# SwiGLU feed-forward: the first gate tile loaded in two halves, one on ACT beside the x transpose, one on SP behind it

## Chip, cores and metric

One core of one Trainium2 chip. The metric is the device time of one execution in microseconds (us). The profile's span (first to last instruction) is some 1.8 us shorter than that time.

## The reference

```python
B, S, D, F = 1, 2048, 512, 1376          # x: (B,S,D); w_gate, w_up: (D,F); w_down: (F,D); all bfloat16
def reference(x, w_gate, w_up, w_down):
    g = silu(x @ w_gate)
    u = x @ w_up
    return (g * u) @ w_down
```

## The kernel before

Everything is computed from a transposed x, so that the features lie on partitions. A "tile" of a weight is 128 of its F columns, held as four slices (dk 0 to 3) of 128 features each, 128 KB in bfloat16. x is taken in four chunks of 512 rows, 512 KB each, which the DMA transposes on the way in. For each chunk and tile, TensorE does four matmuls for the gate and four for the up product (128x128 weights, 512 columns), ACT takes the SiLU of the first, DVE multiplies. Ten matmuls on constants come ahead of all that, to bring TensorE's clock up while the first loads are under way.

The loads, in order of issue; `load_w` takes a range of slices:

```python
N_WARM = 10
...
def load_w(eng, w, base, f0, f1, k0=0, k1=KD): ...   # slices k0..k1 of columns f0..f1, one DMA
...
o = load_x("sp", 0)                       # 512 KB, DMA transpose
for dk in range(KD):
    got_x[0, dk] = o
for a, b in ((0, 1), (1, 2), (2, 4), (4, 7), (7, NFT)):
    g = load_w("act" if a == 0 else "sp", w_gate, 0, a * P, min(b * P, F))
    u = load_w("sp", w_up, UPH, a * P, min(b * P, F - 32))
    for ft in range(a, b):
        for dk in range(KD):
            got_g[ft, dk], got_u[ft, dk] = g, u
# ... rest of up, x chunks 1 to 3, w_down: all on SP
op("act", lambda e: e.activation(adummy[:, 0:4], zero_c, ACT.Silu), inc=False)
for i in range(N_WARM):
    op("pe", lambda e: e.matmul(banks[7][:, :], lhsT=ones_w, rhs=ones_m, start=True, stop=True), inc=False)
...
def mm_g(n, c, ft, dk):
    deps = [got_x[c, dk], got_g[ft, dk]]
    if dk == 0 and n >= NG:
        deps.append(silus[n - NG])
    return mm_k(psG[n % NG], ft * P, c, dk, deps)     # mm_u likewise, with got_u
```

So the first gate tile goes out whole on ACT at the same moment as the x transpose on SP; everything else follows x on SP.

## Time and profile before

| | before |
|---|---|
| time, median of 3 runs | 122.46 us (122.28 to 122.61) |
| span of the profiled run | 120.4 us |
| TensorE busy | 116.4 us, 97% |
| DMA engines busy | in the first 24 us, then only stores |
| first real matmul | 5.18 us after the span's start |

The chain of waits that ended last says what the time is made of (columns: start in us, length in us, what):

```profile
...
0.73 4.40 DMA xT_sb<-in_x_dram
...
5.18 72.69 PE bank L165 x336
...
79.73 38.21 PE bank L246 x187
...
```

Once x has landed at 5.14 us, matmul follows matmul to the end: 336 for gate and up in 72.69 us, which is 216 ns each. A change of the loads can move the time only through the start at 5.18 us, or by making holes just after it.

The timeline before the first matmuls (start, length, engine, line, operation; for SPq and ACTq the length is that of the issue, not of the transfer):

```profile
...
0.73 1.41 SPq L123 DMA_TRANSPOSE xT_sb<-in_x_dram  x1
0.74 0.42 ACTq L131 DMA_DIRECT2D w_sb<-in_w_gate_dram  x1
...
0.77 3.65 PE L162 MATMUL bank<-const-bfloat16-1.0 128*128 128x512 bf16 x10 [0.77 <-PEq L301]
...
2.00 0.15 PEld L162 LDWEIGHTS bank<-const-bfloat16-1.0 128*128 128x128 bf16 x1 [0.28 <-issue]
2.20 0.91 SPq L131 DMA_DIRECT2D w_sb<-in_w_up_dram  x1
2.43 0.15 PEld L162 LDWEIGHTS bank<-const-bfloat16-1.0 128*128 128x128 bf16 x1 [0.27 <-issue]
...
3.17 0.49 SPq L131 DMA_DIRECT2D w_sb<-in_w_gate_dram  x1
...
5.18 4.06 PE L165 MATMUL bank<-xT_sb,w_sb 128*128 128x512 bf16 x18 [0.77 <-DMA xT_sb<-in_x_dram]
...
6.26 0.60 ACT L184 ACTIVATE sg_sb<-bank 128x512 f32<-128x512 f32 x1 [3.57 <-PE bank L165]
...
7.99 0.60 ACT L184 ACTIVATE sg_sb<-bank 128x512 f32<-128x512 f32 x1 [1.13 <-PE bank L165]
...
```

The first SP issue behind x took 0.91 us, the later ones about 0.5. Weight loads (PEld) come one per matmul: those of the warm-up are first 0.43 us apart (2.00, 2.43, ...), and by the end 0.22, so TensorE's clock rose to its full rate near 3.4 us. The SiLUs of the first tiles, at 6.26 and 7.99, are 1.73 us apart, eight matmuls at 216 ns: no hole.

In the DMA view of single issues, the gate tile on ACT landed 2.4 us after its issue (3.14 us), x 4.4 us after (5.14), the first up tile 3.5 us after, the second gate tile at 6.16. The gate tile is there two microseconds before it can be used.

### The profile page before, as it was taken

The page shows a single profiled execution, that of the slowest core. Times are in us where ns is not written, and L with a number is a line of the kernel's source. Part 1 is how long each engine was busy: PE and PEld are TensorE (multiplying, and loading weights), DVE is VectorE, ACT ScalarE, POOL GpSimd, SP SyncE. Part 2 cuts the span into 40 slices and gives each one's busy share as a digit, 9 for nine tenths or more (in the row PEclk, how much of TensorE's full clock was granted, in tenths as well). Part 3 has the DMA queues.
Part 4 walks back from the last instruction along what each step waited for, and adds up shares of the span by engine and source line. Part 5 has one row for each costly group of instructions (what it writes and reads, how often), then busy time and mean ns, then how long its engine had stood idle before and what let it go on. Part 6 is the DMA issues. An engine that isn't in the chain of part 4 may idle for free.

```text
span 120.4 us, 1381 instructions
## 1 busy us (share of the span) xinstructions
PE 116.4 (97%) x549; PEld 53.0 (44%) x549; DVE 43.8 (36%) x64; ACT 30.2 (25%) x51; POOL 0.2 (0%) x4
## 2 busy tenths in 40 slices
PE   7799999999999999999999999999999999999991
PEld 2244444444444444444444444444444444444470
DVE  0024433444433444433444433466332233224230
ACT  4033233353233363233363233320000000000001
POOL 0000000000000000000000000000000000000000
DMA  3999999900000000000000000000211211121121
GB/s 82 270 299 369 264 227 288 306 4 0 0 0 0 0 0 5 0 0 3 3 0 0 0 0 0 5 0 0 87 44 44 87 44 46 58 75 44 44 74 57
DMA packets 17990, 8.51 MB, mean 71 GB/s; under 512 B 11360, under 2 KB 17984, under 8 KB 17984
## 3 DMA queue, kind: packets, MB, share of 16 engines
q1 hardware_dynamic: 17312, 8.23, 25.0%
q10 hardware_dynamic: 672, 0.20, 0.7%
q8 instruction: 4, 0.07, 0.3%
q14 instruction: 2, 0.02, 0.1%
HBM read 4.23 MB, written 2.10 MB: 53 GB/s over the span
## 4 chain that ended last, share of the span: by engine, by line
PE 94%; DMA 4%; ACT 0%; issue 0%
PE bank L165 60%; PE bank L246 32%; DMA xT_sb<-in_x_dram 4%; PE bank L220 2%; ACT o_sb L253 0%
## 5 line engine op out<-in xcount | busy, mean ns | idle before, releaser
L165 PE MATMUL bank<-xT_sb,w_sb 128*128 128x512 bf16 x336 | 72.7, 379 | 0.8 <-DMA xT_sb<-in_x_dram 0.8
L165 PEld LDWEIGHTS bank<-xT_sb,w_sb 128*128 128x128 bf16 x336 | 32.8, 98 | 40.7 <-DMA xT_sb<-in_x_dram 1.3
L187 DVE TENSOR_TENSOR hT_sb<-sg_sb,bank 128x512 bf16<-128x512 f32 x40 | 27.5, 688 | 44.7 <-PE bank L165 44.6
L246 PE MATMUL bank<-wd_sb,hT_sb 128*128 128x512 bf16 (+3 forms) x187 | 38.3, 366 | 0.0
L184 ACT ACTIVATE sg_sb<-bank 128x512 f32<-128x512 f32 x40 | 23.8, 596 | 43.5 <-PE bank L165 43.5
L246 PEld LDWEIGHTS bank<-wd_sb,hT_sb 128*128 128x128 bf16 (+1 forms) x187 | 18.2, 98 | 20.2 <-issue 0.4
L254 DVE CAST o_sb<-bank 128x512 bf16<-128x512 f32 (+1 forms) x16 | 10.8, 674 | 23.7 <-PE bank L246 23.7
L253 ACT ACTIVATE o_sb<-bank 128x256 bf16<-128x256 f32 x1 | 0.4, 384 | 38.9 <-PE bank L246 38.9
L211 DVE TENSOR_TENSOR hT_sb<-sgx_sb,bank 32x512 bf16<-32x512 f32 x4 | 2.8, 693 | 4.9 <-ACT sgy_sb L209 4.9
L162 PE MATMUL bank<-const-bfloat16-1.0 128*128 128x512 bf16 x10 | 3.6, 538 | 0.8 <-PEq L301 0.8
L208 ACT ACTIVATE sgx_sb<-bank 32x512 f32<-32x512 f32 x4 | 2.4, 588 | 4.5 <-PE bank L165 4.5
L226 DVE TENSOR_TENSOR hT_sb<-sgy_sb,bank 64x512 bf16<-64x512 f32 x4 | 2.7, 685 | 0.1
L162 PEld LDWEIGHTS bank<-const-bfloat16-1.0 128*128 128x128 bf16 x10 | 1.2, 131 | 2.7 <-issue 2.6
L209 ACT ACTIVATE sgy_sb<-bank 64x512 f32<-64x512 f32 x4 | 2.4, 589 | 0.0
L220 PE MATMUL bank<-xT_sb,w_sb 128*64 128x512 bf16 x16 | 1.9, 382 | 0.0
L158 ACT ACT_TABLE_LOAD x1 | 1.3, 1283 | 1.2 <-PEq L301 1.2
L220 PEld LDWEIGHTS bank<-xT_sb,w_sb 128*64 128x64 bf16 x16 | 0.8, 109 | 1.0 <-issue 0.4
L158 ACT ACTIVATE act_dummy<-const-float32-0.0 128x4 f32<-128x4 f32 x1 | 0.2, 206 | 0.0
L301 POOL MEMSET const-bfloat16-1.0<- 128x1 bf16 x1 | 0.1, 101 | 0.0
L301 POOL MEMSET const-uint8-127<- 128x1 uint8 x1 | 0.1, 101 | 0.0
L301 POOL MEMSET const-float32-0.0<- 128x1 f32 x1 | 0.1, 98 | 0.2 <-issue 0.2
L301 POOL MEMSET const-float32-1.0<- 128x1 f32 x1 | 0.1, 98 | 0.0
## 6 DMA issues: line engine op xcount, KB each, us to landing
out_dram<-o_sb SPq DMA_DIRECT2D x15, 128.0 KB, 1.7
wd_sb<-in_w_down_dram SPq DMA_DIRECT2D x1, 1280.0 KB, 7.1
w_sb<-in_w_gate_dram SPq DMA_DIRECT2D x1, 480.0 KB, 5.9
w_sb<-in_w_up_dram SPq DMA_DIRECT2D x1, 448.0 KB, 6.0
w_sb<-in_w_gate_dram SPq DMA_DIRECT2D x1, 384.0 KB, 4.6
w_sb<-in_w_up_dram SPq DMA_DIRECT2D x1, 384.0 KB, 5.1
w_sb<-in_w_up_dram SPq DMA_DIRECT2D x2, 128.0 KB, 3.2
w_sb<-in_w_gate_dram SPq DMA_DIRECT2D x1, 256.0 KB, 3.9
```

Of the source, the lines that this page charges most:

```text
L158: op("act", lambda e: e.activation(adummy[:, 0:4], zero_c, ACT.Silu), inc=False)
L162: op("pe", lambda e: e.matmul(banks[7][:, :], lhsT=ones_w, rhs=ones_m, start=True, stop=True), inc=False)
L165: return op("pe", lambda e: e.matmul(bank[:, :], lhsT=w_sb[:, dk, col0:col0 + P], rhs=xT_sb[:, dk, c * SC:(c + 1) * SC], start=(dk == 0), ...
L184: s = op("act", lambda e: e.activation(sg_sb[n % NSG][:, :], psG[n % NG][:, :], ACT.Silu), [g, mults[n - NSG] if n >= NSG else None])
L187: mults.append(op("dve", lambda e: e.tensor_tensor(hT_sb[:, ft, c * SC:(c + 1) * SC], sg_sb[n % NSG][:, :], psU[n % NU][:, :], ALU.mult), ...
L208: op("act", lambda e, c=c: e.activation(sgx_sb[c][96:128, :], psX[64:96, :], ACT.Silu), [xm], inc=False)
L209: rest_a[c] = op("act", lambda e, c=c, y0=y0, y1=y1: e.activation(sgy_sb[c][y0:y1, :], psX[0:64, :], ACT.Silu), [xm])
L211: rest_x[c] = op("dve", lambda e, c=c: e.tensor_tensor(hT_sb[64:96, NFF, c * SC:(c + 1) * SC], sgx_sb[c][96:128, :], psX[96:128, :], ALU.m ...
L220: ym = op("pe", lambda e, pi=pi, dk=dk, c=c, y0=y0, y1=y1: e.matmul(psY[pi][y0:y1, :], lhsT=w_sb[:, dk, YC0:YC0 + 64], rhs=xT_sb[:, dk, c ...
L226: rest_y[c] = op("dve", lambda e, pi=pi, c=c, y0=y0, y1=y1: e.tensor_tensor(hT_sb[0:64, NFF, c * SC:(c + 1) * SC], sgy_sb[c][y0:y1, :], ps ...
L246: om = op("pe", lambda e, K=K, fk=fk: e.matmul(bank[:, 0:ncol], lhsT=hT_sb[0:K, fk, t * P:(t + 1) * P], rhs=wd_sb[0:K, fk, c0:c0 + ncol], ...
L254: return op("dve", lambda e: e.tensor_copy(ob[:, a:b], bank[:, a - c0:b - c0]), deps)
```

## The change

The gate tile's bytes use the same DMA engines as x while x is what TensorE waits for. The intent is to take half of them out of x's way: the half that is needed first (features 0 to 255) stays on ACT, the other half comes on SP right behind x, then the up tile.

```diff
-        for a, b in ((0, 1), (1, 2), (2, 4), (4, 7), (7, NFT)):
-            g = load_w("act" if a == 0 else "sp", w_gate, 0, a * P, min(b * P, F))
+        early = load_w("act", w_gate, 0, 0, P, 0, KD // 2)
+        late = load_w("sp", w_gate, 0, 0, P, KD // 2, KD)
+        up = load_w("sp", w_up, UPH, 0, P)
+        for dk in range(KD):
+            got_g[0, dk], got_u[0, dk] = early if dk < KD // 2 else late, up
+        for a, b in ((1, 2), (2, 4), (4, 7), (7, NFT)):
+            g = load_w("sp", w_gate, 0, a * P, min(b * P, F))
             u = load_w("sp", w_up, UPH, a * P, min(b * P, F - 32))
```

## The prediction

> **What bounds the kernel now.** TensorE. The page gives PE 97% busy; the chain of waits is 94% PE, 4% one DMA: the first x transpose, issued at 0.73 us, landed at 5.14. After 5.18 the chain is unbroken matmul: 336 at the gate/up line in 72.69 us (216 ns each), 16 for the rest in 1.85, 187 down in 38.21. So only the PE start and holes in the first tiles can move.
>
> **What the change does.** The first gate tile (128 KB) goes out today on ACT at 0.74 and lands 2.4 us later, at 3.16 (DMA issues by tile) with 2 us to spare; but its bytes share the DMA engines with x. In the windows table the engines are full (share 1.2 to 1.3, 270 to 290 GB/s) from 2.2 us to 5.8 us. The Trainium skill ("DMA: Bandwidth & Descriptors", section "Issuing engines are not separate DMA queues") says transfers from ACT and SP run on the same 16 engines and interleave; the trace agrees: the total stays near 280 GB/s with and without the ACT transfer. The change takes 64 KB out of x's way and puts it behind x on SP. Estimate: 65.5 kB / 280 GB/s = 0.23 us, so x lands near 4.9 and PE starts near 4.95.
>
> **What it costs.** One more SP issue, 0.49 to 0.51 us (timeline), so every later SP issue moves back about 0.5 us. Deadlines, with four matmuls = 0.865 us and PE starting at 4.95:
> - late half: needed at 4.95 + 0.43 = 5.38. Before, 128 KB behind x landed 0.56 after x (5.70); 64 KB should land 0.3 after it, near 5.2. Slack 0.15 us.
> - first up tile: needed at 5.81. The bytes ahead of it are unchanged, so 5.7. Slack 0.1 us.
> - gate 1, up 1: landed 6.17, 6.60, needed 6.68, 7.55: fine, also 0.3 us later.
> - gates 2 and 3 (256 KB): landed 8.15, needed 8.41. Around 6.0 to 6.4 us the engines are not full (share 0.84, 138 GB/s), so this transfer is probably bound by its issue; if all 0.5 us came through, it would land at 8.65 and open a hole of 0.2 us, giving the gain back.
> - ups 2 and 3: landed 8.9, needed 9.27; a similar risk. Later tiles have over 1 us.
>
> **Sum.** Gain 0.23 us at the start, minus about 0.08 us for the chance that part returns as a hole: 122.46 - 0.15 = 122.3 us. The range, 121.95 to 122.65, is mostly the runs' spread. Faster by over 2%: 1%; within 2%: 98%; slower by over 2%: 1%.
>
> **What would show each step.** (1) x landing at 4.85 to 5.0, its time to landing down from 4.4 to about 4.2 us; (2) first gate/up matmul at 4.9 to 5.05; (3) SP issues from the first up tile on 0.4 to 0.55 us later; (4) the waits list: no PE wait on w_sb of over 0.1 us in the first 1.0 us of matmuls; perhaps one of 0.1 to 0.3 us near 8.4 us for gates 2 and 3; (5) the chain after that the same 112.8 us.
>
> **What would make it wrong.** x may be bound not by the shared engines but by its own issue (1.41 us) and transposing, and then lands at 5.14 as before: no gain, and the late half and up tile have more slack. The late half or the up tile may land later than the byte count says, since the first issue behind x took 0.91 us, not 0.5; each would stall PE by 0.1 to 0.4 us, and the run would be 122.5 to 122.8.

## The result, and the profile after

| | before | after |
|---|---|---|
| time, median | 122.53 us (122.28 to 122.67, 4 runs) | 122.48 us (122.23 to 122.56, 4 runs) |
| ratio | | 0.9995, interval 0.9971 to 1.0018 |
| x lands, us after its issue | 4.4 | 4.0 |
| first real matmul | 5.18 us | 4.99 us |
| first SiLU | 6.26 us | 6.59 us |

A ratio is the mean time of one kernel's runs over that of the other's runs of the same rounds, so not quite the ratio of the medians. Executions over 1.5% slower than the fastest of the same kernel are left out of the means. The interval spans 0.36 us down to 0.22 us up: the two kernels can't be told apart. Yet x landed 0.4 us earlier (the view of x's first issue, after):

```profile
...
DMA to landing us min/median/max: 4.0/4.0/4.0
```

The profiled runs took 122.17 us (before, a run outside the four listed) and 122.56 us (after). The chain of waits after:

```profile
...
0.77 4.43 PE bank L167 x10
5.20 73.01 PE bank L170 x336
...
80.05 38.21 PE bank L251 x187
...
```

The DMA of x has gone from the chain. In its place stand the ten warm-up matmuls, 4.43 us of them, where those of before took 3.65; and the 336 real ones took 73.01 us, not 72.69. The timeline after:

```profile
...
0.73 0.42 ACTq L131 DMA_DIRECT2D w_sb<-in_w_gate_dram  x1
0.73 1.40 SPq L123 DMA_TRANSPOSE xT_sb<-in_x_dram  x1
...
2.19 0.57 SPq L131 DMA_DIRECT2D w_sb<-in_w_gate_dram  x1
...
2.82 0.45 SPq L131 DMA_DIRECT2D w_sb<-in_w_up_dram  x1
...
3.31 0.51 SPq L131 DMA_DIRECT2D w_sb<-in_w_gate_dram  x1
...
4.14 0.15 PEld L167 LDWEIGHTS bank<-const-bfloat16-1.0 128*128 128x128 bf16 x1 [0.28 <-issue]
...
4.99 4.37 PE L170 MATMUL bank<-xT_sb,w_sb 128*128 128x512 bf16 x17
5.42 0.15 PEld L170 LDWEIGHTS bank<-xT_sb,w_sb 128*128 128x128 bf16 x1 [0.28 <-DMA w_sb<-in_w_gate_dram]
...
5.84 0.15 PEld L170 LDWEIGHTS bank<-xT_sb,w_sb 128*128 128x128 bf16 x1 [0.28 <-issue]
...
6.17 2.90 PEld L170 LDWEIGHTS bank<-xT_sb,w_sb 128*128 128x128 bf16 x14 [0.17 <-issue]
6.59 0.60 ACT L189 ACTIVATE sg_sb<-bank 128x512 f32<-128x512 f32 x1 [3.90 <-PE bank L170]
...
8.31 0.60 ACT L189 ACTIVATE sg_sb<-bank 128x512 f32<-128x512 f32 x1 [1.13 <-PE bank L170]
```

Weight loads are still 0.42 us apart at 5.42 and 5.84: in this run TensorE's clock rose near 6.0 us, not near 3.4. So the warm-up matmuls ended only at about 5.0 us, after x, and the first real matmuls ran at half speed. From first matmul to first SiLU it took 6.59 - 4.99 = 1.60 us, before 6.26 - 5.18 = 1.08. The early start gained 0.19 us, the slow clock took 0.52, and the sum, 0.33, is the difference between the two SiLUs and between the two profiles' ends. After that the SiLUs are 1.72 us apart: no hole.

Does the change cause the late rise, or chance? The Trainium skill ("TensorE: Matmul & The Clock Gate", section "What's actually happening") describes a clock gate that goes from half to full rate after a window of about 3.4 us has been busy enough, and says that the window is free-running and does not start with the kernel. The two rates agree with these traces (427 and 216 ns per matmul); that the moment varies from run to run is seen below. The views print a granted clock of 1.00 throughout the first 6 us, but that is no measurement: they print 1.00 wherever the trace has no clock record. The packed trace's own clock records (not shown by a view) begin at 6.06 us here and at 5.67 in the repeat below, where the spacing also puts the rise; the profile of before has none. Eleven of the fourteen traces have such records, and all but the last one of each, cut off by the end, last 3.41, 6.83, 112.64, 116.05 or 119.47 us, each a whole multiple of 3.413, as a free-running window would make them. By these records, or by the spacing where there are none, the rise lay between 3.4 and 6.7 us with the load order of before and with that of the change alike (later only in the run with eight warm-up matmuls), so it is chance and not the change.

The SP issues: the first one behind x took 0.57 us (before 0.91), so the second gate tile was issued at 3.31 us instead of 3.17, 0.14 us later, not 0.5.

### The profile page after: what moved, and what is told of

The parts are those of the page before. It is cut to its first block, busy times and chain, and to the rows that moved or that the text cites. A ratio compares the mean times of both kernels' runs of the same rounds, so it can differ in the third digit from the quotient of the medians.

```text
span 120.8 us, 1382 instructions
## 1 busy us (share of the span) xinstructions
PE 117.5 (97%) x549; PEld 53.4 (44%) x549; DVE 43.8 (36%) x64; ACT 30.2 (25%) x51; POOL 0.2 (0%) x4
## 4 chain that ended last, share of the span: by engine, by line
PE 97%; ACT 0%; issue 0%
PE bank L170 60%; PE bank L251 32%; PE bank L167 4%; PE bank L225 2%; ACT o_sb L258 0%
## 5 line engine op out<-in xcount | busy, mean ns | idle before, releaser
L167 PE MATMUL bank<-const-bfloat16-1.0 128*128 128x512 bf16 x10 | 4.4, 629 | 0.8 <-PEq L306 0.8
```

## Experiments

Theory 1: x does land earlier; the gain is hidden by TensorE's clock. Theory 2: the warm-up matmuls stand in the way. Theory 3: x's earlier landing was chance. And a fourth: the gain comes back as holes. Each run below was made with the kernel before on the same chip. "Held" kernels are an instrument, described with the first of them.

### The changed kernel again

No edit.

> The changed kernel again, unchanged, for more runs. Theory 1 (the gain is real but hidden by the TensorE clock at the start, whose rise to full speed came near 3.4 us in the profile of before and near 6.0 us in the profile of after): runs spread over about 0.5 us, the fastest run near 121.9 (0.4 below the fastest of before, 122.28), the mean 0.15 to 0.25 us below before. Theory 2 (the ten warm-up matmuls at the slow clock, 4.43 us, now end after x has landed and take the gain in every run): fastest run not under 122.15, mean within 0.1 us of before. Theory 3 (x does not land earlier in most runs, the profile of after was lucky): x lands at 5.0 to 5.2 us in this profile.

Measured: 122.08, 122.28, 122.30, 122.32, 122.80, 122.87, mean 122.44 us; before, 11 runs of 122.06 to 123.02, ratio 1.0001 (0.9967 to 1.0035). x landed 4.1 us after its issue, so theory 3 is weakened. The clock rose near 5.7 us, and again the warm-up matmuls (4.42 us) were in the chain. The mean shows no gain, as theory 2 expected, and the fastest run is no faster than before's 122.06 (though 122.08 lies just under the 122.15 that theory 2 allowed); the spread of 0.8 us is more than the 0.5 that theory 1 expected, and before has it too (0.96 us).

### Fewer warm-up matmuls

```diff
-N_WARM = 10
+N_WARM = 8
```

> The changed kernel with 8 warm-up matmuls instead of 10: at the slow clock they end near 4.2 us, ahead of x at 4.73. Theory 1: mean equal to the repeat within 0.1 us. Theory 2: 0.15 us or more below the repeat, PE starts real work at x's landing (4.75 to 4.85 us) whatever the clock. If instead the idle gap delays the clock's rise, the mean is 0.1 us or more above the repeat.

Measured: four fast runs of 121.98, 122.13, 122.49 and 122.99 us, mean 122.40, ratio 0.9996 (0.9956 to 1.0036); two more, 124.15 and 124.55, were slow, and the profile fell in the first of them. The mean of the four equals the repeat's 122.44 within 0.1 us, as theory 1 said; theory 2 asked for 0.15 us less. No comparison of times is taken from the profile, only what it shows of the clock (weight loads after x):

```profile
...
5.25 0.13 PEld L170 LDWEIGHTS bank<-xT_sb,w_sb 128*128 128x128 bf16 x2 [1.82 <-DMA xT_sb<-in_x_dram]
...
8.64 0.15 PEld L170 LDWEIGHTS bank<-xT_sb,w_sb 128*128 128x128 bf16 x1 [0.28 <-issue]
9.06 4.85 PEld L170 LDWEIGHTS bank<-xT_sb,w_sb 128*128 128x128 bf16 x23 [0.27 <-issue]
```

x landed late in this run (4.5 us after issue), TensorE stood idle for 0.92 us after its eight warm-up matmuls, and the weight loads stayed 0.42 us apart until 9.06 us. Theory 2's cure fails in the fast runs, and a hole ahead of the rise can cost more than it saves. An estimate from the traces: counted back in steps of 3.41 us from the rise, the stretch from 2.23 to 5.65 us held the whole 0.92 us of idle time, and without it the rise would have come at 5.65. In the other thirteen traces, counted the same way, the stretches ahead of the rise with up to 0.72 us of idle time were followed by the full clock and those with 0.89 us or more were not. Had x landed at 4.73, the hole would have been 0.4 us and harmless by this count; x was late here (4.5 us after issue).

### The clock taken out: both kernels held back

To take the clock out of the comparison, the x and gate loads wait for four ACT activations, which moves everything by 3.6 us (4.4 had been expected, and so a time near 126.8), and 24 warm-up matmuls keep TensorE busy, so that the clock has risen before x lands. The same edit was made to the kernel before and to the changed one:

```diff
-N_WARM = 10
+N_WARM = 24
+        op("act", lambda e: e.activation(adummy[:, 0:4], zero_c, ACT.Silu), inc=False)   # moved up from below the loads
+        for i in range(4):
+            hold = op("act", lambda e, i=i: e.activation(adelay[:, i, :], ones_m, ACT.Silu))
-                return dma(eng, ... xf[t0:t1, :]))
+                return dma(eng, ... xf[t0:t1, :]), [hold])        # load_w likewise
```

> The kernel before with the first x and gate loads held back about 4.4 us by four ACT activations, and 24 warm-up matmuls, so that in every run the clock has risen before x lands. It takes the clock's lottery away. x lands about 4.4 us after its issue, near 9.5 us; runs near 126.8 us with a spread of under 0.2 us if the clock causes the spread; a spread of 0.4 us as before if it does not.

> The same hold on the changed kernel. Theory 1 and 2: 0.3 to 0.45 us below the held kernel before, x lands 4.0 us after its issue instead of 4.4. Theory 3, or a hole later in the first tiles (late half, up tile, gates 2 and 3): within 0.1 us of it, and in case of a hole a PE wait on w_sb of 0.2 us or more in the waits list.

Measured: held before 125.77 to 125.87 (6 runs, mean 125.83), held changed 125.63 to 125.92 (6 runs, mean 125.75); the kernel before itself, in the same rounds, 122.06 to 123.02. The spread fell from 0.96 us to 0.10 and 0.29. The edit takes away the clock's share and also covers part of x's own jitter (the held kernel before had its 24 warm-up matmuls end at 8.91 us, x landing at 8.83), so the fall is not all the clock's. With 22 warm-up matmuls (next section, and the last) the held kernel before spread over 0.33 and 0.39 us, the plain one beside it over 0.48 and 0.68; but those are four runs against nine and eleven, and fewer runs spread less by themselves.

The difference of 0.08 us was expected to be 0.3 to 0.45. x landed at 4.5 and 4.2 us after issue. The SiLUs of the held changed kernel show where some of it went:

```profile
...
8.55 0.11 PEld L172 LDWEIGHTS bank<-xT_sb,w_sb 128*128 128x128 bf16 x2 [0.59 <-DMA xT_sb<-in_x_dram]
...
9.53 2.27 PEld L172 LDWEIGHTS bank<-xT_sb,w_sb 128*128 128x128 bf16 x12 [0.43 <-DMA w_sb<-in_w_up_dram]
9.63 0.60 ACT L191 ACTIVATE sg_sb<-bank 128x512 f32<-128x512 f32 x1 [5.33 <-PE bank L172]
...
11.47 0.60 ACT L191 ACTIVATE sg_sb<-bank 128x512 f32<-128x512 f32 x1 [1.24 <-PE bank L172]
...
13.19 0.60 ACT L191 ACTIVATE sg_sb<-bank 128x512 f32<-128x512 f32 x1 [1.13 <-PE bank L172]
...
```

Between the first two SiLUs lie 1.84 us, then 1.72: a hole of 0.11 us, at the weight load that waits for the first up tile. That tile landed at 9.48 us and its weight load began at 9.53; it was due four matmuls after 8.55, at 9.41. The late half landed at 8.84 us, needed at 8.98: no hole, and 1.08 us from first matmul to first SiLU, as before.

### Held with 22 warm-up matmuls, and without the holes

With 24, a late rise lets the warm-up matmuls run past x's earlier landing. So both again with 22, and a version in which the first gate and up tile read only the early half's weights, which takes away the waits for the late half and the up tile while all loads are still made:

```diff
         def mm_g(n, c, ft, dk):
+            if n == 0:
+                return mm_k(psG[0], 0, 0, dk, [got_x[0, dk], early], dk % 2)   # slice dk % 2 of the gate
         def mm_u(n, c, ft, dk):
+            if n == 0:
+                return mm_k(psU[0], 0, 0, dk, [got_x[0, dk], early], dk % 2)
```

> The held kernel before with 22 warm-up matmuls instead of 24, so that even with the latest rise of the clock they end before x lands. Within 0.1 us of the first held kernel before (125.82 us); real matmuls start at x's landing, near 8.85 us; spread again under 0.2 us.

> The held changed kernel with 22 warm-up matmuls. If the warm-up matmuls still stood in the way in some of the runs with 24 (their spread was 0.29 us against 0.10): 0.2 to 0.35 us below the held kernel before of this call, spread under 0.2 us. If holes in the first tiles are what eats the gain: still about 0.1 us below, and PE waits on the late half and the first up tile of 0.1 us or so each.

> As the held changed kernel, but the first gate and up tile are computed with the early half's weights for all four slices and for both, so neither the late half nor the first up tile is waited for (the result is wrong on purpose; the loads are still made). Theory holes: 0.1 to 0.2 us below the held changed kernel, so 0.3 us or so below the held kernel before, the whole of what x lands earlier. Theory no holes: equal to the held changed kernel within 0.05 us.

Measured, same chip: held before 125.70 to 126.03 (4 runs, mean 125.84); held changed 125.65 to 126.37 (5 runs, median 125.91, mean 125.94); without holes 125.57 to 125.82 (4 runs, mean 125.68), its result wrong. The chains of the first and the last:

```profile
...
4.33 4.35 DMA xT_sb<-in_x_dram
...
8.72 72.69 PE bank L167 x336
...
83.27 38.21 PE bank L248 x187
...
```

```profile
...
4.33 4.15 DMA xT_sb<-in_x_dram
...
8.52 72.72 PE bank L173 x336
...
83.09 38.21 PE bank L258 x187
...
```

In these two profiles real work started at 8.72 and 8.52 us, and the chains end the same 112.8 us later; 0.20 us at the start is still 0.18 us where the down matmuls start (83.27 and 83.09). Across all runs, without the waits the mean is 0.16 us below the held kernel before (0.3 was expected). It is 0.25 us below the held changed kernel by the medians (0.1 to 0.2 was expected). With the waits, the held changed kernel is not below the held one before (0.10 us above here, where either theory had it below; 0.08 below with 24). So what x gains is there, 0.2 us or so, and in these runs at most half of it was left once the first up tile has been waited for. The differences are as small as the spread of these few runs; the direction is supported by the holes in the trace, the exact share is not settled.

The profiled run of the held changed kernel with 22 was its slowest, 126.37 us. Its windows of time show a stall of the DMA engines in the middle of x (columns: stretch in us, its length, busy time of the engines, granted clock, DMA share, GB/s):

```profile
...
5.80:6.20 0.40, 0.40 (x2) 0.15 (x1) 0.00 (x0) 0.00 (x0) 0.00 (x0) 1.00 1.04 231
6.20:6.80 0.60, 0.60 (x3) 0.25 (x2) 0.00 (x0) 0.00 (x0) 0.00 (x0) 1.00 1.36 101
...
```

From 6.2 to 6.8 us only 101 GB/s were moved. x landed 4.6 us after issue, and gates 2 and 3 landed at 12.74 us, with a wait of 0.6 us for them in the list of waits. The same kind of stall appears in two more profiles: both halves on ACT (143 GB/s over 0.6 us) and eight warm-up matmuls (102 to 191 over 1.0 us). All three are versions of the changed kernel, none of the six with the first gate tile whole, too few to say whether the change brings it on. If it does, that is one more way for the gain to be lost; its cause is open.

### The late half from ACT

The added SP issue is taken away: the late half goes out on ACT behind three more activations, meant to put it 1.6 us after x.

```diff
-        late = load_w("sp", w_gate, 0, 0, P, KD // 2, KD)
+        for i in range(4, 7):
+            hold2 = op("act", lambda e, i=i: e.activation(adelay[:, i, :], ones_m, ACT.Silu))
+        late = dma("act", ... w_gate[2 * P:4 * P, 0:P] ..., [hold2])
```

> The held changed kernel with the late half issued on ACT about 1.6 us after x (behind three more ACT activations), so that no SP issue is added: the first up tile is again the first SP issue behind x. Theory holes by the added SP issue: no wait for the first up tile and at least 0.05 us below the held changed kernel. If the late half now shares the engines with the last of x again, x lands 0.1 to 0.2 us later than in the held changed kernel and the two come out equal.

Measured: 126.12 to 126.56 us (4 runs, mean 126.35), half a microsecond above the held kernel before. x landed at 4.2, so the late half did not slow it, but the chain has the late half in it:

```profile
...
4.80 1.68 ACT act_delay L148 x3
...
6.50 2.99 DMA w_sb<-in_w_gate_dram
...
```

The activations put its issue at 6.50 us, 2.2 us after x and not 1.6, and it landed 3.0 us later, at 9.48. From the first real matmul (8.63) to the first SiLU (10.17) it took 1.54 us instead of 1.08: a hole of 0.46 us, the whole loss. The first up tile, again the first SP issue behind x, landed at 9.30, ahead of its need at 9.50, as theory holes had said. On SP, issued at 5.79, it had also landed 3.0 us after its issue. So the late half lands some 3.0 us after its issue, on either queue (3.3 to 3.5 where a DMA stall slowed x). The same figure holds for the first up tile wherever the late half goes ahead of it on SP (2.9 to 3.0); as the first SP issue behind x it took 3.5, both here and in the kernel before, where it landed 0.6 us behind x. So the change seems to have turned the up tile from a load that waits for bytes ahead of it into one that waits for its issue. In the held kernel without holes the engines are not full there: 154, 123 and 169 GB/s in the three 0.2 us stretches from 8.0 us.

### How much on ACT costs x how much

Four held kernels with 22 warm-up matmuls on one chip: before again; both halves on ACT; the whole gate tile behind x on SP; and gate and up tile both on ACT.

```diff
 halves_held:     late = load_w("act", w_gate, 0, 0, P, KD // 2, KD)      # was "sp"; on the changed kernel
 behind_held:     g = load_w("sp", w_gate, ...)                            # was "act" for a == 0; on before
 up_on_act_held:  u = load_w("act" if a == 0 else "sp", w_up, ...)         # was "sp"; on before
```

> The held kernel before with 22 warm-up matmuls once more, to stand beside the next three on the same chip. 125.7 to 125.9 us; x lands 4.35 to 4.5 us after its issue.

> Held; the first gate tile is cut in two halves, but both go out on ACT ahead of x's end, so the same 128 KB shares the engines with x. If moving 64 KB out of x's way is what makes x land earlier, x lands as in the held kernel before (4.35 to 4.5 us after its issue) and the time is within 0.1 us of it. If the smaller transfer itself does it (a shorter first transfer on ACT), x lands at 4.0 to 4.2 and the time is 0.15 us or more below.

> Held; the whole first gate tile goes behind x on SP, nothing on ACT. Sharing theory: x lands another 0.2 to 0.3 us earlier, 3.75 to 4.0 us after its issue; but the gate lands 0.5 us behind it, so the first real matmul starts at 8.8 to 9.0 us, where the held kernel before starts near 8.75, and the first up tile, another 0.5 us later, is just in time: 0 to 0.3 us above the held kernel before. If x is bound by its own transposing, x lands at 4.1 or later.

> Held; the first up tile goes on ACT too, behind the gate tile, so 256 KB share the engines with x instead of 128. Sharing theory: x lands 0.4 to 0.6 us later than in the held kernel before, 4.8 to 5.1 us after its issue, and the time is 0.4 to 0.6 us above it, with no holes afterwards. If x is not slowed by bytes on ACT: x lands at 4.35 to 4.5 and the time is equal within 0.1 us.

| held kernel | on ACT beside x | x lands after | runs, us |
|---|---|---|---|
| before, again | 128 KB | 4.5 us | 125.86, 125.89, 125.97, 126.25 |
| both halves on ACT | 2 x 64 KB | 4.8 us (DMA stall in the profile) | 126.12 to 126.23, and 127.92 |
| gate behind x | nothing | 4.2 us | 126.17, 126.19, 126.39, 126.53 |
| gate and up on ACT | 2 x 128 KB | 4.9 us | 126.28 to 126.47, and 127.93, 127.98 |

The three runs near 127.9 us need a word. The profiles of both kernels fell in such runs and show the clock dropping again (here gate and up on ACT; the third number from the end of a line is the granted clock):

```profile
...
9.00:10.40 1.40, 1.16 (x6) 0.57 (x7) 0.00 (x0) 0.08 (x1) 0.00 (x0) 1.00 1.20 319
10.50:13.80 3.30, 3.30 (x9) 1.22 (x8) 0.69 (x1) 0.78 (x2) 0.00 (x0) 0.50 1.11 366
14.00:15.00 1.00, 1.00 (x6) 0.45 (x5) 0.34 (x1) 0.03 (x1) 0.00 (x0) 1.00 1.11 370
...
```

The clock had risen early, 22 warm-up matmuls ended near 7.1 us, and TensorE stood idle for 2.12 us; some 1.2 us after work resumed, the clock went to half for about 3.4 us. This is a flaw of the instrument: with the earliest rise, 22 are too few for an x that lands late. Leaving these three out, the means are 126.19 us (halves on ACT), 126.32 (behind x), 126.38 (gate and up) against 125.99 (before).

Taking a quarter megabyte onto ACT slows x, as sharing says: 0.4 us for the added 128 KB, and 0.39 us in the mean time, expected 0.4 to 0.6. Taking the last 64 KB away did not speed it up further: 4.2 us with nothing on ACT, 4.0 to 4.2 with one half in the five undisturbed profiles of it, so the expected 3.75 to 4.0 failed, and what came is the other branch, x bound by itself ("x lands at 4.1 or later"). The windows of time show why one half is free. First with nothing on ACT, in four stretches; then with one half (without holes) and with the whole tile (before), over the same 1.6 us at once:

```profile
...
5.40:5.80 0.40, 0.40 (x4) 0.16 (x3) 0.00 (x0) 0.00 (x0) 0.00 (x0) 1.00 0.06 13
5.80:6.20 0.40, 0.40 (x3) 0.17 (x2) 0.00 (x0) 0.00 (x0) 0.00 (x0) 1.00 0.69 166
6.20:6.60 0.40, 0.40 (x3) 0.20 (x2) 0.00 (x0) 0.00 (x0) 0.00 (x0) 1.00 1.17 248
6.60:7.00 0.40, 0.40 (x3) 0.20 (x2) 0.00 (x0) 0.00 (x0) 0.00 (x0) 1.00 1.27 272
...
```

```profile
...
5.40:7.00 1.60, 1.60 (x9) 0.61 (x7) 0.00 (x0) 0.00 (x0) 0.00 (x0) 1.00 1.07 235
...
```

```profile
...
5.40:7.00 1.60, 1.60 (x8) 0.74 (x7) 0.00 (x0) 0.00 (x0) 0.00 (x0) 1.00 1.02 222
...
```

x alone ramps up: 13, 166, 248, 272 GB/s. By 7.0 us that is 0.4 us times their sum, 280 KB, all of it x. With one half on ACT, which has landed by 6.46 us, it is 1.6 us times 235 GB/s, 376 KB, of which 376 - 66 = 310 KB are x. With the whole tile, landed by 6.69, it is 1.6 us times 222 GB/s, 355 - 131 = 224 KB. So the first half rides where x does not yet fill the engines; the second half costs x 86 KB of headway, at 290 GB/s 0.3 us. (These are sums over single profiles: x had 280 and 286 KB in two more held profiles with one half, 205 and 207 in two more with the whole tile, so the first 64 KB may cost or help x by a tenth of a microsecond.)

The packets by queue say it more directly. Queue 1 is SP's, with x at its head, queue 10 is ACT's; the lines are of the stretch from 5.00 to 5.95 us, with one half on ACT (without holes), with the whole tile (before), and with nothing (columns: packets, MB, share of the engines' time):

```profile
...
q10 hardware_dynamic: 272, 0.07, 36.4%
q1 hardware_dynamic: 92, 0.02, 10.6%
```

```profile
...
q10 hardware_dynamic: 219, 0.06, 32.1%
```

```profile
...
q1 hardware_dynamic: 101, 0.03, 11.3%
```

In the packed traces x's first packet moves at 5.74 us with nothing on ACT, at 5.74 to 5.80 in all held profiles whose first ACT load is a half tile, and at 5.98 to 6.10 where it is a whole one (2.12 to 2.15 against 2.46 without the hold). So what the change wins is an earlier start of x, 0.2 to 0.4 us (64 KB at 280 GB/s take 0.23). Of the half tile 32 to 45 of 66 KB go ahead of x's first packet, of the whole tile 73 to 101 of 131. Why x begins later behind the whole tile, rather than taking turns from 5.74 us on, is open.

Both halves on ACT came out 0.2 us above before, where equal was expected if only bytes count. Its one profile had a stall of the DMA engines in x (143 GB/s from 6.6 to 7.2 us), so whether two transfers on ACT cost x more than one of the same size stays open. x's first packet moved early there (5.75 us), but the times of its five other runs rule out that cutting the tile is by itself what helps.

The gate behind x shows the other end: x early, but the gate lands 0.5 us behind it, real work starts at 9.19 us instead of 8.87, and the run is 0.33 us longer, at the upper end of what was expected.

None of these versions beats the kernel before.

## Why the prediction was right, and where not

**No change of time: right.** 122.3 us was predicted, 122.48 measured, both kernels within the noise of each other. The predicted gain of 0.15 us did not show in ten runs of the changed kernel; noise does not exclude it. With a few tenths at stake in 122 us, "within 2%" was safe whatever the mechanism; that the number itself came out close is partly luck, since what ate the gain in the two plain profiles, the clock, was not in the sum.

**x lands earlier: right, sized well.** Predicted "near 4.9" by 64 KB at 280 GB/s = 0.23 us. Undisturbed profiles have 4.0 to 4.2 us after issue with one half on ACT against 4.4 to 4.5 with the whole tile, 0.2 to 0.5 us. The share of the engines is the cause, with a limit that the prediction did not see: the first 64 KB are free, because x's first packet moves no later with them than without (5.74 to 5.80 us against 5.74, held).

**"Every later SP issue moves back about 0.5 us": wrong.** From the second gate tile on it was 0.14 us (3.31 against 3.17). The 0.91 us of the first issue behind x was not a cost of the 128 KB it carried: with the whole gate tile there instead and nothing on ACT, the same 128 KB took 0.64 us. In the undisturbed profiles this issue took 0.86 to 0.99 us with a whole tile or two beside x on ACT, and 0.57 to 0.67 with less (both halves on ACT, in the profile with a stall, 0.56); why it follows x's headway was not tested. The feared hole at gates 2 and 3 thus never came in the undisturbed profiles (landing at 8.25 us instead of 8.65), but for 0.03 us in the run without the other holes.

**First up tile, "bytes ahead of it are unchanged, so 5.7", slack 0.1: this step failed.** Its issue moved back by 0.62 us (2.82 against 2.20), and it lands 2.9 to 3.0 us after issue: at 5.74 and 5.82 us in the plain profiles. Held, it came 0.11 us too late. Under "what would make it wrong" the prediction did name a late up tile, but for another reason, a first issue of 0.91 us; that issue took 0.57. The prediction subtracted 0.08 us for a hole at gates 2 and 3; a hole of about that size lay at the first up tile.

**"Four matmuls = 0.865 us" and "the chain after that the same 112.8 us": wrong in the two plain profiles.** Both had the slow clock past x's landing, and the chain from the end of the warm-up was 113.06 us (5.20 to 118.26) in the first and 112.87 (5.19 to 118.06) in the repeat, whose clock rose earlier. The warm-up, which the prediction left out (it ended at 4.42 in the profile of before), ended near 5.0 and set the start in both. One profile of before, with an early rise, had been taken for the rule.

**"The range is mostly the runs' spread": right, without its cause.** The clock's rise accounts for the 0.33 us between the ends of the two profiles, and with it taken out the spread was smaller in each of the three sets of rounds (0.96 us to 0.10, 0.48 to 0.33, 0.68 to 0.39), though over fewer runs each time; what is left is, as far as the traces show, x's own jitter and the DMA stalls. The prediction knew nothing of the clock.

So x's gain of 0.2 to 0.3 us goes two ways: with a late clock the warm-up matmuls hold the start at 5.0 us and what is gained runs at half speed; with an early one, seen only in the held kernels, the first up tile is late by a tenth. What remains is below what ten runs can show.

## What to carry to other kernels

Before taking bytes out of a critical transfer's way, see when its first packet moves and when it really fills the engines: what goes ahead of that is free (64 KB here). Then put every load behind it on a list with its deadline and its issue time, since a load pushed back one place can become bound by its issue though no byte ahead of it has changed. And where a gain is a few tenths of a microsecond, look first at how long the clock takes to rise in several profiles: one profile may show a start that most runs don't have, and a start held back on purpose makes a quieter instrument, provided that no idle time is left ahead of it.

## What the Trainium skill lacked or had wrong

- "TensorE: Matmul & The Clock Gate", section "HAM oscillation — how this bites in real kernels", puts its rule at "no PE-idle gaps >~3.4µs". Here an idle time of 2.12 us (gate and up on ACT) and one of 2.16 us (both halves on ACT) were followed by about 3.4 us at half clock, and such runs were 1.5 to 1.7 us longer than the others of the same kernel. Idle times of 1.30 us (without holes) and 1.50 us (gate behind x) were not followed by a drop.
- The same page ("What you observe") gives the moment of the rise as varying by about 500 ns from run to run, though further on it has a kernel with 6, 11 or 14 slow matmuls. Here the larger figure holds: in these profiles it lay near 3.4 us (before), 5.7 and 6.0 (changed), all with the first warm-up matmul at 0.77 us; with an idle 0.92 us in between, at 9.06.
- No page that was used says that the trace may hold no clock record over the slow start (the first one is at 6.06 us in the profile of after, and three of the fourteen traces have none), so that a view that takes no record for full rate reads 1.00 while matmuls came every 427 ns. The clock page's section "Seeing it yourself" does warn that the clock's events can be unreliable.
- "DMA: Bandwidth & Descriptors", section "Issuing engines are not separate DMA queues", holds as far as it goes: with the engines full, 128 KB more on ACT delayed x by 0.4 us. It lacks how the interleaving begins: 64 KB on the other queue left x's first packet where it was (5.74 to 5.80 us, 5.74 with nothing there) and cost it nothing, 128 KB in one load put it off to 5.98 to 6.10.
- No page that was used has the DMA stalls of 0.6 to 1.0 us at 101 to 191 GB/s in the middle of x's transfer (elsewhere mostly 250 to 290), seen in three of the fourteen profiles; they move a start by 0.4 us and are as large as the effect under study.
